# Eight output buffers instead of three, one raw-V buffer instead of two, and relu and output scaling free to run on VectorE or ScalarE, in a fused attention and expert kernel

## The chip, the cores and the metric

The kernel runs on one core of a Trainium2 chip. The metric is the device time of one execution in microseconds (us), as the median of the runs. The span in a profile is about 2 us shorter than the time of the same run. Runs whose time lies over 1.5% above the fastest of the same kernel are marked slow.

A ratio is the mean time of one kernel's fast runs over the mean of the other's fast runs of the same rounds, so it is not quite the quotient of the medians that are quoted.

## The reference, cut to what matters

```python
# q, k, v: (8, 8, 576, 64).  Attention in a window of 32 to each side
scores = scale * q @ k^T;  scores = where(|i - j| <= 32, scores, -1e9)
x = (softmax(scores) @ v)  ->  (8, 576, 512)
# one expert of eight for each of the 8 batches
logits = x.mean(axis=1) @ w_gate          # (8, 8)
e_idx  = argmax(logits)                   # the batch's expert
out[b] = gate_w[b] * (relu(x[b] @ w1[e]) @ w2[e])   # w1: 512x1024, w2: 1024x512
```

The expert is known only when a batch's attention is done, so its weights are loaded in the middle of the work. While they load, the attention of the next batch runs.

## The kernel before

A planner in the kernel simulates the engines with a duration for each piece of work and emits the instructions in the order that it finds. On the chip each engine then works its queue in that order; only what a piece needs makes it wait: its data, a free buffer and, as e8 below shows, the semaphores of transfers. A piece planned for `BOTH` goes to whichever of VectorE (`DVE`) and ScalarE (`ACT`) the planner finds better.

The profile's names: PE is TensorE, PEld its weight load, POOL GpSimd, SP SyncE; ACTq and SPq are the issuing of transfers by ScalarE and SyncE. `bank` is a matmul's result, `qT`, `kT` and `xT` are transposed q, k and attention outputs, `E` the exponentials, `vaug` the V that the attention matmuls read, `vraw` V as it was loaded, `w` the expert's weights, `hT` the hidden layer after relu, `gwb` the gate weight and `osb` the outputs.

```python
vraws = buffers("vraw", [P, NVS + 1, D], FP32, 2)
buffers("osb", [P, DM], FP32, 3)                     # outputs on their way to memory
...
# exponentials (line 468) on ScalarE, masks (474 to 487) on VectorE
plan.add("ACT", 0.63, f"X{sn}", ex, ...)
plan.add("DVE", 0.47 if half == 0 else 0.4, f"M{sn}", msk, ...)
...
# first expert matmul (line 664), 16 times per batch; then relu
nc.scalar.activation(h_of[(b, ft)][:, 288*c : 288*c + 288], bank_of.pop(gn)[:, 0:288], ACTF.Relu)
...
# second expert matmul (lines 700 and 706), 5 outputs per batch; then the scaling (line 726)
nc.scalar.activation(osb[:, 0:w], bank_of.pop(f"2{b}{i}")[:, 0:w], ACTF.Copy,
                     bias=0.0, scale=tiny("gwb", [P, 1], FP32, b))
...
# the store is issued from ScalarE's queue too (line 737)
nc.scalar.dma_start(out[b, 128*i : 128*i + 128, :], osb)
```

The softmax here doesn't subtract the row's maximum and nothing guards it: scores larger than these inputs give would overflow.

## Time and profile before

| | kernel before |
|---|---|
| time, median of 3 runs | 305.97 us (305.24 to 307.08) |
| span of the profiled run | 302.7 us |
| TensorE busy, and so not busy | 231.4 us, 71.3 us |
| mean granted TensorE clock | 0.861 |
| VectorE busy, ScalarE busy | 168.9 us, 163.5 us |

The lines of the profile stand in the prediction.

### The profile page before, as it was taken

How to read it: one execution, taken by the hardware profiler on the slowest of the kernel's cores; microseconds unless marked ns; L12 is line 12 of the kernel's file. 1: busy time of each engine (PE TensorE's matmuls, PEld its weight loads, DVE VectorE, ACT ScalarE, POOL GpSimd, SP SyncE). 2: the span in 40 equal slices, each digit the busy share in tenths (PEclk: the TensorE clock that was granted, in tenths of full speed). 3: DMA queues.
4: the chain of work that ended last, by engine and by line, in shares of the span. 5: the costliest groups of instructions: out<-in, count | busy, mean ns of one | idle time of the engine just before them, and what ended most of it. 6: DMA issues, size and time to landing. Idle time of an engine off the chain costs nothing.

```text
span 302.7 us, 6131 instructions
## 1 busy us (share of the span) xinstructions
PE 231.4 (76%) x2432; PEld 177.3 (59%) x2432; DVE 168.9 (56%) x453; ACT 163.5 (54%) x320; POOL 68.4 (23%) x83
## 2 busy tenths in 40 slices
PE   1475878995899649995699729993599929975990
PEld 1374756854796339854496429852497518833840
DVE  7889992475459735685458925686277525400000
ACT  8692923572578255681577425681466535631640
POOL 4536060091106400091004600082002200010000
PEclk9996975999599958997599958997599977995798
DMA  7879999099997997089942996079101970089021
GB/s 248 281 214 393 298 197 269 30 180 264 348 344 166 241 362 223 1 157 235 384 131 38 241 322 228 2 142 226 68 2 17 212 192 17 2 160 239 35 106 53
DMA packets 26637, 55.00 MB, mean 182 GB/s; under 512 B 2064, under 2 KB 12272, under 8 KB 24560
## 3 DMA queue, kind: packets, MB, share of 16 engines
q0 software_dynamic: 2304, 16.78, 29.4%
q1 hardware_dynamic: 18656, 28.39, 27.5%
q10 hardware_dynamic: 5648, 9.44, 8.5%
q8 instruction: 19, 0.31, 0.4%
q14 instruction: 10, 0.08, 0.1%
HBM read 61.94 MB, written 9.44 MB: 236 GB/s over the span
## 4 chain that ended last, share of the span: by engine, by line
PE 49%; DMA 31%; DVE 8%; ACT 5%; issue 4%; ACTq 0%
DMA out_dram<-osb 28%; PE bank L664 25%; PE bank L700 9%; PE bank L513 5%; PE bank L391 4%; PE bank L549 3%; DMA w<-in_moe_w_dram 3%; ACT E L468 2%; ACT osb L726 2%; PE bank L574 1%; DVE E L487 1%; ACT kT L307 1%; DVE qT L305 1%; PE bank L439 1%; PE bank L596 1%
## 5 line engine op out<-in xcount | busy, mean ns | idle before, releaser
L664 PE MATMUL bank<-xT,w 128*128 128x288 f16 x512 | 90.3, 333 | 12.6 <-ACT osb L726 7.3
L664 PEld LDWEIGHTS <-w 128*128 128x128 f16 x512 | 66.5, 151 | 23.6 <-issue 9.0
L682 ACT ACTIVATE hT<-bank 128x288 f16<-128x288 f32 x128 | 51.8, 411 | 37.0 <-PE bank L664 31.5
L513 PE MATMUL bank<-vaug,E 128*128 128x65 f16 x576 | 33.9, 210 | 39.4 <-ACT E L468 30.2
L700 PE MATMUL bank<-w,hT 128*128 128x512 f16 x256 | 63.6, 379 | 0.0
L726 ACT ACTIVATE osb<-bank,gwb 128x512 f32<-128x512 f32 (+1 forms) x40 | 25.7, 642 | 64.6 <-DMA out_dram<-osb 53.5
L487 DVE TENSOR_TENSOR E<-E,mask 128x384 f16<-128x384 f16 (+1 forms) x64 | 34.6, 550 | 38.9 <-ACT E L468 38.9
L513 PEld LDWEIGHTS <-E 128*128 128x128 f16 x576 | 29.2, 109 | 43.6 <-issue 32.5
L634 POOL DMA_DIRECT2D w<-in_moe_w_dram x8 | 4.7, 585 | 176.8 <-DVE gw L627 135.5
L468 ACT ACTIVATE E<-bank 128x512 f16<-128x512 f32 x72 | 41.1, 596 | 3.5 <-PE bank L439 1.4
L330 POOL CAST qkb<-raw 128x1152 bf16<-128x1152 f32 x32 | 37.7, 1212 | 13.5 <-DMA raw<-in_k_dram 7.4
L305 DVE COPY qT<-bank 64x512 bf16<-64x512 bf16 (+1 forms) x46 | 35.3, 774 | 2.1 <-PE bank L391 0.6
L700 PEld LDWEIGHTS <-hT 128*128 128x128 f16 x256 | 22.8, 98 | 18.3
L391 PE MATMUL bank<-id_bf,qkb 128*128 128x128 bf16 x288 | 25.4, 234 | 10.2 <-POOL qkb L330 7.6
L391 PEld LDWEIGHTS <-qkb 128*128 128x128 bf16 x288 | 20.4, 105 | 15.2 <-POOL qkb L330 8.1
L535 DVE TENSOR_TENSOR xs<-bank,linv 128x256 f16<-128x256 f32 x64 | 27.1, 424 | 2.2
L439 PEld LDWEIGHTS <-kT 128*128 128x128 bf16 x288 | 20.3, 103 | 10.2 <-issue 4.7
L439 PE MATMUL bank<-qT,kT 128*128 128x128 bf16 x288 | 24.6, 230 | 1.9 <-DVE qT L305 1.3
L307 ACT COPY kT<-bank 128x512 bf16<-128x512 bf16 (+1 forms) x26 | 18.4, 736 | 9.7 <-PE bank L391 9.6
L305 DVE COPY xT<-bank 128x512 f16<-128x512 f16 (+1 forms) x23 | 8.8, 384 | 25.9 <-PE bank L549 25.8
L365 POOL CAST vaug<-vraw 128x1152 f16<-128x1152 f32 (+1 forms) x16 | 18.9, 1236 | 6.8 <-DMA vraw<-in_v_dram 6.8
L533 DVE RECIPROCAL linv<-bank 128x4 f32<-128x4 f32 (+1 forms) x80 | 13.9, 174 | 8.6 <-PE bank L513 8.1
(61 smaller groups left out, 176.8 us busy)
## 6 DMA issues: line engine op xcount, KB each, us to landing
w<-in_moe_w_dram POOLq DMA_DIRECT2D x16, 1024.0 KB, 11.9
raw<-in_q_dram SPq DMA_DIRECT2D x16, 576.0 KB, 4.6
raw<-in_k_dram SPq DMA_DIRECT2D x16, 576.0 KB, 9.6
out_dram<-osb ACTq DMA_DIRECT2D x32, 256.0 KB, 10.5
out_dram<-osb ACTq DMA_DIRECT2D x8, 128.0 KB
vraw<-in_v_dram SPq DMA_DIRECT2D x8, 0.2 KB, 11.2
vraw<-in_v_dram SPq DMA_DIRECT2D x8, 8.0 KB, 10.0
vraw<-in_v_dram SPq DMA_DIRECT2D x1, 24.0 KB
```

The lines of the kernel that those rows point to most:

```text
L305: nc.vector.tensor_copy(dst, src)
L330: nc.gpsimd.tensor_copy(t, raw[(b, quad, name)].rearrange("p h j d -> p j h d"))
L391: nc.tensor.transpose(pv[:, j - j0, :], raw[(b, quad, name)][:, j], id_bf)
L439: nc.tensor.matmul(dst, qkT[(b, a, "k")][:, k0 : k0 + P], qkT[(b, a, "q")][:, :, k0 : k0 + 64], start=(m == 0), stop=True, skip_group_chec ...
L468: nc.scalar.activation(dst, src, ACTF.Exp, bias=0.0, scale=0.125)
L487: nc.vector.tensor_tensor(ev, ev, mask[:, 1:2].unsqueeze(1).broadcast_to([P, 2, m, 64]), ALU.mult)
L513: nc.tensor.matmul(bank[:, hp * 65 : hp * 65 + 65], E_of[b][:, h, c0 : c0 + P], va_of[b][:, late, slot, 0:65], start=(hp == 0 and n == 0), ...
L535: nc.vector.tensor_tensor(xv[:, par], hv[:, :, 0:64], linv.to_broadcast([n, 4, 64]), ALU.mult)
L664: nc.tensor.matmul(bank[:, 0:288], w_of[b][0].rearrange("p t (c n) -> p t n c", c=P)[:, dt, ft], xT_of[b][:, dt, 288 * c : 288 * c + 288], ...
L682: nc.scalar.activation(h_of[(b, ft)][:, 288 * c : 288 * c + 288], bank_of.pop(gn)[:, 0:288], ACTF.Relu,)
L700: nc.tensor.matmul(bank, h_of[(b, ft)][:, 128 * i : 128 * i + 128], w2s[:, ft, :], start=(ft == 0), stop=(ft == NFT - 1),)
L726: nc.scalar.activation(osb[:, 0:w], bank_of.pop(f"2{b}{i}")[:, 0:w], ACTF.Copy, bias=0.0, scale=tiny("gwb", [P, 1], FP32, b),)
```

## The change

The intent is to take ScalarE's wait for output stores away with five more buffers, to make room for them by giving up one buffer of raw V, and to let VectorE, which had as much time to spare, take part of relu and scaling. The planner's assumption of how long a store holds its buffer is lengthened as well.

```diff
-                over = end + 2.6
+                over = max(end + 2.6, min(dma_at + 0.7, end + 10.0))
...
-    vraws = buffers("vraw", [P, NVS + 1, D], FP32, 2)
+    vraws = buffers("vraw", [P, NVS + 1, D], FP32, 1)
...
-    buffers("osb", [P, DM], FP32, 3)
+    buffers("osb", [P, DM], FP32, 8)
...
+                    if op.eng == "DVE":
+                        nc.vector.tensor_scalar_max(dst, src, 0.0)
+                    else:
+                        nc.scalar.activation(dst, src, ACTF.Relu)
-                plan.add("ACT", 0.42, "R" + gn, relu,
+                plan.add(BOTH, {"DVE": 0.38, "ACT": 0.42}, "R" + gn, relu,
...
+                if op.eng == "DVE":
+                    nc.vector.tensor_scalar_mul(osb[:, 0:w], src, gwb)
+                else:
+                    nc.scalar.activation(osb[:, 0:w], src, ACTF.Copy, bias=0.0, scale=gwb)
-            plan.add("ACT", 0.69 if i < 4 else 0.43, f"V{b}{i}", evac,
+            plan.add(BOTH, {"DVE": 0.62, "ACT": 0.7} if i < 4 else {"DVE": 0.36, "ACT": 0.44}, f"V{b}{i}", evac,
```

In the changed kernel's profile the second expert matmuls are lines 702 and 708, relu is line 685 (VectorE) and 687 (ScalarE), the scaling 730 and 732, and the store 740 and, for a batch's fifth output, 742.

## The prediction

> **What bounds the kernel now.** I began with the page: the share of each engine, the strip of 40 slices, then the chain that ended last.
>
> ```profile
> PE 231.4 (76%) x2432; PEld 177.3 (59%) x2432; DVE 168.9 (56%) x453; ACT 163.5 (54%) x320; POOL 68.4 (23%) x83
> ...
> PE 49%; DMA 31%; DVE 8%; ACT 5%; issue 4%; ACTq 0%
> DMA out_dram<-osb 28%; PE bank L664 25%; PE bank L700 9%; PE bank L513 5%; PE bank L391 4%; PE bank L549 3%; DMA w<-in_moe_w_dram 3%; ACT E L468 2%; ACT osb L726 2%; PE bank L574 1%; DVE E L487 1%; ACT kT L307 1%; DVE qT L305 1%; PE bank L439 1%; PE bank L596 1%
> ```
>
> No engine is full, TensorE is nearest, and 28% of 302.7 us, about 85 us, is time in which the chain sits on an output store. A store should release nobody in a hurry, so I asked the view of waits who waits for it.
>
> ```profile
> ACT osb L726 <- DMA out_dram<-osb: 53.5, 13, 6.7
> DVE E L487 <- ACT E L468: 38.9, 15, 6.2
> ...
> PE bank L513 <- ACT E L468: 30.2, 9, 5.6
> DVE xT L305 <- PE bank L549: 25.8, 22, 6.2
> ...
> PE bank L664 <- ACT osb L726: 7.3, 4, 2.5
> ...
> PE bank L664 <- ACT hT L682: 0.4, 1, 0.4
> ```
>
> ScalarE stands 53.5 us, in 13 waits, before the output scaling (line 726), because its buffer is still being stored. There are three buffers and five outputs per batch, so outputs 4 and 5 of a batch wait for stores 1 and 2, and a 256 KB store takes a median of 10.5 us to land. ScalarE works in program order, so the exponentials of the next batch (line 468), which have their data, stand behind that wait; VectorE's masks and TensorE's attention matmuls then wait for them. The last line matters as well: TensorE hardly ever waits for relu.
>
> The timeline from 202 to 220 us (the sixth batch's experts start there) shows one such stop. Columns: start, duration, engine, line, operation, and in brackets the idle time before it.
>
> ```profile
> 202.29 0.69 ACT L726 ACTIVATE osb<-bank,gwb 128x512 f32<-128x512 f32 x1 [0.53 <-PE bank L700]
> ...
> 207.99 0.69 ACT L726 ACTIVATE osb<-bank,gwb 128x512 f32<-128x512 f32 x1 [3.94 <-DMA out_dram<-osb]
> ...
> 209.30 0.60 PE L513 MATMUL bank<-vaug,E 128*128 128x65 f16 x8 [2.89 <-ACT E L468]
> ...
> 214.54 0.47 ACT L726 ACTIVATE osb<-bank,gwb 128x256 f32<-128x256 f32 x1 [5.38 <-DMA out_dram<-osb]
> ...
> 215.55 0.60 PE L513 MATMUL bank<-vaug,E 128*128 128x65 f16 x8 [5.65 <-ACT E L468]
> ...
> 215.96 3.50 PE L664 MATMUL bank<-xT,w 128*128 128x288 f16 x16
> ```
>
> TensorE loses 2.89 and 5.65 us, and the first expert matmuls (line 664) start only at 215.96. The same stop comes at every batch. Last, I cut this stretch into windows (columns: start and end, length, busy us per engine, granted clock, DMA share, GB/s).
>
> ```profile
> 205.40:206.40 1.00, 1.00 (x18) 0.84 (x16) 1.00 (x1) 0.00 (x0) 0.61 (x1) 1.00 1.26 285
> 206.40:209.30 2.90, 0.02 (x1) 0.03 (x1) 1.98 (x7) 1.17 (x2) 0.00 (x0) 0.87 1.01 229
> ...
> 211.00:215.50 4.50, 0.00 (x0) 0.00 (x0) 0.00 (x0) 0.96 (x2) 0.00 (x0) 0.50 0.38 135
> 215.50:217.60 2.10, 2.05 (x15) 1.56 (x15) 1.36 (x4) 1.05 (x3) 0.00 (x0) 0.50 0.09 25
> ...
> 219.90:223.00 3.10, 3.10 (x47) 3.06 (x46) 2.42 (x9) 1.94 (x5) 0.00 (x0) 1.00 0.00 0
> ```
>
> The clock falls to 0.50 in the stop and is only back at 1.00 by 220: the stop is paid a second time. It also shows that VectorE was still busy until about 208.3, which limits what can be won.
>
> **What the Trainium skill says.** "TensorE: Matmul & The Clock Gate", Part 1, says that the clock is halved after an idle window of about 3.4 us and full again after about as long a busy one. The trace agrees: 0.50 in the stop, and on the chain 16 matmuls of line 664 take 3.31 us from 216.15 (207 ns each) and 12 take 1.51 us from 220.93 (126 ns each). "DMA: Bandwidth & Descriptors", Issuing engines are not separate DMA queues, says all queues run on the same 16 engines and interleave; so a store shares with the weights and inputs. The trace agrees: 10.5 us median when they run, as little as 2.0 us at best. "VectorE: DVE Perf Modes", Why PSUM operands drop a tier, says an fp32 PSUM operand runs at the plain rate on VectorE. The trace fits: 128x256 out of fp32 PSUM takes 424 ns (line 535) while a 128x512 fp16 copy out of PSUM also takes 424 ns (line 305). So VectorE is no cheaper place for relu or scaling. "SBUF — State Buffer", Who interferes with whom, says VectorE and GpSimd share a port pair that one holds alone. The trace agrees: the mask of line 487 takes 1.30 us at 201.40 beside GpSimd's casts, 0.35 us at 207.56 after them.
>
> **The change part by part.** *Eight output buffers.* Output n waits for store n-8, over a batch back, 30 us against 10 to 13 us of landing: all 53.5 us of these waits should go. What it is worth on the path I read stop by stop, as how much earlier the experts' matmuls could start. Two other things bound that: VectorE's work queue, and the weights, whose first half lands 8.2 to 9.9 us after issue. At 216: masks and copies are done at 208.3, two groups of attention matmuls follow, so the start moves to about 209.5, a gain of 6.4 us; the weights, issued at 197.7, are there by 206.5. At 249 (weights issued at 232.84, landing near 241.6): start near 242, gain 7. At 180: about 6, by likeness. At 148 (eight of these matmuls were done before its second wait): 4.5. At 111 (masks done at 104.3): 5.5. At 76.7 (eight done before): TensorE lost 1.38 and 2.23 us, so 3.7. In the last batch the first eight start at 274.48 when the weights land, which stays; the wait until 277.82 after them goes, about 2.5. Sum 35.6 us of the 53.5.
>
> *Clock.* Six stops are followed by about 16 matmuls at half rate; at 207 to 240 ns instead of 126 that is 1.3 to 1.8 us, six times 8 to 11 us. A pause of some 2 us before the attention matmuls stays (206.4 to 208.5), so I count 6.5 us.
>
> *Relu and scaling on both engines.* 128 relus of 411 ns and 40 scalings of 642 ns are on ScalarE, 77.5 us. On VectorE I estimate, from 424 ns for 256 elements and one element per 0.96 GHz cycle (that clock is the "VectorE: DVE Perf Modes" page's), 157 ns fixed: 457 ns for a relu and 690 ns for a 512-wide scaling. Each moved instruction saves ScalarE what it costs VectorE. TensorE waits 0.4 us for relu, so this alone gives nearly nothing; scaling on VectorE can even get between two masks. I count 0, plus or minus 4 us, as the order of the two queues will be planned anew.
>
> *One buffer for raw V.* The load of V for the next batch must wait for GpSimd's cast of this one. In the steady part the cast comes right after the weights are issued (130.4, 164.5, 199.1 us) and its next one a batch later, so a load of about 11 us has 25 us: hidden. At the start it is not: the second V load is issued at 13.01 us, the first cast ends at 15.9, and SyncE's later loads stand behind it in order. About 3 us of delay in the second batch's casts, where TensorE already waits 5.9 us; I charge 2 us.
>
> Sum: 35.6 + 6.5 - 2 = 40 us, so 306 - 40 = 266 us.
>
> **The rivals.** *The wait was hidden anyway, or the weights take its place.* For: they land on the same saturated DMA engines, and at 274.48 they are already the releaser. Against: at 216 they had 9 us of slack. If all periods were bound by issue to landing, I would gain only some 20 us: 285. *DMA becomes the bound.* The shares of the queues, 29.4 + 27.5 + 8.5% of 302.7 us, are 198 us, 24.7 per batch. Before, a period was about 34 us; at 27 us it is 92% full, and with one V buffer the input loads move into the burst right after the weights' issue. That could cost 1 to 2 us a period: 272 to 280. *VectorE becomes the bound.* It is full from 197.4 to 208.3 already; three scalings of 0.69 us there would delay the masks by 2 us a batch, 14 us in all: 280. Against: the planner puts an instruction where the queue is shorter. *Everything opens up.* All 53.5 us plus 11 of clock: 242 us, but TensorE's 26.6 busy us of the 35.1 us from 193.9 to 229.0 and VectorE's queue speak against it.
>
> **Range and chances.** The stop is real and repeated, and five new buffers remove it without new work, so faster is nearly certain. The two DMA and VectorE rivals pull up more than a better plan pulls down. Predicted 266 us, 8 in 10 between 256 and 281; faster 0.96, same 0.03, slower 0.01.
>
> **What would show it.** In the changed profile the wait of output scaling on its store should be below 3 us and its 28% of the chain gone; TensorE's share should be near 85%, the mean clock above 0.90 (0.861 now), and expert matmuls should start every 27 to 28 us instead of 30 to 36. Some 40 to 70 relus should be VectorE's, near 0.46 us, with their wait still nil. The wait of TensorE for GpSimd's casts near 30 us should grow by about 2. I am wrong if the new plan puts another wait between experts: for weights (first landing above 12 us), or for VectorE.

## More of the kernel before

"Busy" counts the time in which an engine had an instruction running, so a matmul at half the clock counts twice as long as at the full clock. That is why the split of TensorE's span into busy and not busy is worth keeping: lost clock is in the first part, waiting is in the second.

## The result, and the profile after

The changed kernel takes 264.25 us (260.86 to 264.82, 3 runs) against 305.97 us, ratio 0.8578 (95% interval 0.8433 to 0.8722): faster, and within 2 us of the predicted 266. The span is 261.9 us and the mean clock 0.942.

The page of the changed kernel: the engines' shares, then the chain that ended last by engine and by line.

```profile
PE 217.2 (83%) x2432; PEld 170.5 (65%) x2432; DVE 204.9 (78%) x524; ACT 131.7 (50%) x249; POOL 68.0 (26%) x80
...
PE 55%; DVE 26%; DMA 6%; issue 5%; ACT 4%; ACTq 1%; POOLq 1%; DVEq 0%
```

The store, 28% of the chain before, is gone, and the view of waits has no line any more for a scaling that waits for a store. But VectorE, 8% of the chain before, is now 26%. In the view of waits these lines lead to it (engine, line and what it waited for; us in all, times, longest):

```profile
ACT E L468 <- PE bank L439: 14.7, 12, 3.4
...
PE bank L439 <- DVE kT L305: 5.4, 4, 2.3
...
PE bank L513 <- DVE vaug L370: 4.7, 4, 2.0
...
PE bank L513 <- ACT E L468: 2.6, 6, 0.7
```

TensorE's attention matmuls (line 513) waited 30.2 us for exponentials before and wait 2.6 us now. A new chain of waits has come: the score matmuls (line 439) wait for VectorE's copy of k, and ScalarE's exponentials wait for those scores.

The groups of relu and scaling in the changed kernel, shapes kept apart (count, busy us, mean ns, idle before):

```profile
L687 ACT ACTIVATE hT<-bank 128x288 f16<-128x288 f32 x72 | 29.5, 412 | 28.5 <-PE bank L664 26.4
L685 DVE TENSOR_SCALAR hT<-bank 128x288 f16<-128x288 f32 x56 | 25.6, 458 | 20.8 <-PE bank L664 19.9
...
L730 DVE TENSOR_SCALAR osb<-bank,gwb 128x512 f32<-128x512 f32 x19 | 14.2, 746 | 7.9 <-PE bank L702 7.8
...
L732 ACT ACTIVATE osb<-bank,gwb 128x512 f32<-128x512 f32 x13 | 8.9, 683 | 1.7 <-PE bank L702 1.7
```

Both jobs take longer on VectorE than on ScalarE. The planner thinks the opposite: 0.38 us for a relu on VectorE and 0.62 us for a scaling.

The timeline shows what that does around the point where the kernel before had its stop (changed kernel, one period; start, duration, engine, line, operation, idle time before it):

```profile
178.05 1.16 DVE L482 TENSOR_TENSOR E<-E,mask 128x128 f16<-128x128 f16 x1
179.13 1.30 DVE L487 TENSOR_TENSOR E<-E,mask 128x384 f16<-128x384 f16 x1
180.35 0.81 DVE L305 COPY kT<-bank 128x640 bf16<-128x640 bf16 x1
181.09 0.74 DVE L730 TENSOR_SCALAR osb<-bank,gwb 128x512 f32<-128x512 f32 x1
...
181.85 0.34 ACTq L740 DMA_DIRECT2D out_dram<-osb  x1
182.24 1.08 ACT L468 ACTIVATE E<-bank 128x512 f16<-128x512 f32 x2 [3.36 <-PE bank L439]
```

```profile
181.31 0.61 PE L439 MATMUL bank<-qT,kT 128*128 128x128 bf16 x8 [2.33 <-DVE kT L305]
```

VectorE works without a pause through masks, a copy of k and a scaling. TensorE stands 2.33 us for the copy of k, which VectorE had put behind two masks of over a microsecond each (GpSimd's casts run beside them, from 177.86 to 181.44 us). ScalarE stands 3.36 us. The profile names the scores as what ended this wait, but ScalarE's store (line 740) is issued at 181.85, as the scaling on VectorE ends (181.09 plus 0.74 us), and it stands in front of the exponentials in ScalarE's queue.

The same 147 us of both kernels as one window, first before and then changed (start and end, length, busy us of TensorE, weight load, VectorE, ScalarE and GpSimd, then clock, DMA share, GB/s):

```profile
75.00:222.00 147.00, 116.27 (x1282) 90.80 (x1282) 91.32 (x226) 80.96 (x169) 33.76 (x37) 0.84 0.72 201
```

```profile
75.00:222.00 147.00, 136.23 (x1660) 109.84 (x1659) 126.60 (x321) 86.85 (x179) 37.28 (x42) 0.99 0.84 224
```

The clock is at 0.99 instead of 0.84, and TensorE is busy for 136 of 147 us instead of 116. Eleven us are still lost here, and VectorE is the busiest of the other engines.

### The profile page after: what moved, and what is told of

Same layout as the page of the kernel before. It is cut to its first block, busy times and chain, and to the rows that moved or that the text cites. A ratio compares the mean times of both kernels' runs of the same rounds, so it can differ in the third digit from the quotient of the medians.

```text
span 261.9 us, 6135 instructions
## 1 busy us (share of the span) xinstructions
PE 217.2 (83%) x2432; PEld 170.5 (65%) x2432; DVE 204.9 (78%) x524; ACT 131.7 (50%) x249; POOL 68.0 (26%) x80
## 4 chain that ended last, share of the span: by engine, by line
PE 55%; DVE 26%; DMA 6%; issue 5%; ACT 4%; ACTq 1%; POOLq 1%; DVEq 0%
PE bank L664 27%; PE bank L702 10%; DMA w<-in_moe_w_dram 6%; PE bank L513 6%; DVE E L487 6%; DVE qT L305 5%; PE bank L549 3%; DVE E L482 3%; PE bank L439 3%; PE bank L391 3%; DVE kT L305 3%; ACT E L468 2%; DVE osb L730 2%; PE bank L708 2%; PE bank L574 2%
## 5 line engine op out<-in xcount | busy, mean ns | idle before, releaser
L664 PE MATMUL bank<-xT,w 128*128 128x288 f16 x512 | 77.6, 301 | 6.3 <-DMA w<-in_moe_w_dram 6.2
L664 PEld LDWEIGHTS <-w 128*128 128x128 f16 x512 | 62.7, 147 | 9.9 <-DMA w<-in_moe_w_dram 6.6
L687 ACT ACTIVATE hT<-bank 128x288 f16<-128x288 f32 x72 | 29.5, 412 | 28.5 <-PE bank L664 26.4
L685 DVE TENSOR_SCALAR hT<-bank 128x288 f16<-128x288 f32 x56 | 25.6, 458 | 20.8 <-PE bank L664 19.9
L513 PE MATMUL bank<-vaug,E 128*128 128x65 f16 x576 | 29.6, 200 | 13.1 <-DVE vaug L370 4.7
L513 PEld LDWEIGHTS <-E 128*128 128x128 f16 x576 | 25.5, 102 | 16.6 <-issue 13.4
L391 PE MATMUL bank<-id_bf,qkb 128*128 128x128 bf16 x288 | 25.8, 234 | 10.3 <-POOL qkb L330 7.3
L305 DVE COPY qT<-bank 64x640 bf16<-64x640 bf16 (+1 forms) x39 | 30.3, 783 | 1.3 <-ACT qT L307 0.3
L307 ACT COPY xT<-bank 128x512 f16<-128x512 f16 (+1 forms) x26 | 13.6, 528 | 18.4 <-PE bank L549 17.7
L307 ACT COPY qT<-bank 64x512 bf16<-64x512 bf16 (+1 forms) x25 | 18.2, 729 | 9.1 <-DVE qT L305 5.6
L730 DVE TENSOR_SCALAR osb<-bank,gwb 128x512 f32<-128x512 f32 (+1 forms) x21 | 15.2, 721 | 8.4 <-PE bank L702 7.8
```

The source lines that it names most:

```text
L305: nc.vector.tensor_copy(dst, src)
L307: nc.scalar.copy(dst, src)
L391: nc.tensor.transpose(pv[:, j - j0, :], raw[(b, quad, name)][:, j], id_bf)
L513: nc.tensor.matmul(bank[:, hp * 65 : hp * 65 + 65], E_of[b][:, h, c0 : c0 + P], va_of[b][:, late, slot, 0:65], start=(hp == 0 and n == 0), ...
L664: nc.tensor.matmul(bank[:, 0:288], w_of[b][0].rearrange("p t (c n) -> p t n c", c=P)[:, dt, ft], xT_of[b][:, dt, 288 * c : 288 * c + 288], ...
L687: nc.scalar.activation(dst, src, ACTF.Relu)
```

## The experiments

Twelve kernels were run, all with correct results. A kernel with eight output buffers and two V buffers could not be built, because the memory of a partition was over-full by 2.3 KB (210.2 of 207.9), so that corner is missing.

**e1: the buffers alone.** Relu and scaling stay on ScalarE; eight output buffers and one V buffer are kept.

```diff
-                plan.add(BOTH, {"DVE": 0.38, "ACT": 0.42}, "R" + gn, relu,
+                plan.add("ACT", 0.42, "R" + gn, relu,
-            plan.add(BOTH, {"DVE": 0.62, "ACT": 0.7} if i < 4 else {"DVE": 0.36, "ACT": 0.44}, f"V{b}{i}", evac,
+            plan.add("ACT", 0.7 if i < 4 else 0.44, f"V{b}{i}", evac,
```

> Changed kernel with relu and output scaling on ScalarE alone again (eight output buffers and one V buffer kept). Theory A (the prediction's: the buffers carry the gain, the second engine is worth 0 plus or minus 4 us): 260 to 268 us, no wait of ScalarE for an output store, relu wait of TensorE below 2 us. Rival B (ScalarE's queue would have become the next bound, so the second engine is needed): over 272 us, with TensorE's expert matmuls waiting for relu or the exponentials. Rival C (VectorE, now 78% busy and 26% of the chain, is the bound that the move made): below 258 us and VectorE's share of the chain back near 10%.

Measured: 252.18 us (251.35 to 253.61), ratio 0.8256 (0.8203 to 0.8308). The range of theory A, 260 to 268 us, is missed. Theory C holds in the time: without the second engine the kernel is about 12 us faster than the changed one by the medians, and 10 us by the ratios (0.8578 - 0.8256 = 0.0322 of 305 us). On the chain its share for VectorE only falls to 23%, not to 10%, so that part of C was wrong. The page and the window of e1:

```profile
PE 215.7 (86%) x2432; PEld 170.1 (68%) x2432; DVE 167.6 (67%) x453; ACT 163.6 (65%) x320; POOL 68.3 (27%) x80
```

```profile
75.00:222.00 147.00, 142.24 (x1714) 113.85 (x1712) 112.06 (x299) 105.42 (x222) 38.77 (x45) 1.00 0.86 229
```

TensorE is busy 142.24 of 147 us, 97%, at the full clock. There is hardly anything left to be won on other engines in this part.

**e2: the V buffer alone.** The kernel before with one line changed.

```diff
-    vraws = buffers("vraw", [P, NVS + 1, D], FP32, 2)
+    vraws = buffers("vraw", [P, NVS + 1, D], FP32, 1)
```

> Kernel before with one raw V buffer and nothing else. Theory A: the V loads are hidden in the steady part and the start loses up to 2 us: 305 to 309 us, the 53 us of waits for stores unchanged. Rival (the later V loads push the input loads into the weights' landing): over 312 us, and the first half of the weights lands later than 10 us after its issue.

Measured: 303.71 us (303.6 to 305.4), ratio 0.9971 (0.9905 to 1.0037): the same, and a little below the 305 us that were expected at least. The waits of ScalarE for stores are 53.7 us, as before. The start lost nothing either: the first weights were issued at 37.76 us, against 38.23 before. The planner, knowing of one buffer, puts the second batch's loads of q and k in front of its V load. With e1 this is a clean pair: the orders of all five queues of e1 and e2 are identical, and only the number of output buffers differs (8 and 3). So the five buffers by themselves are worth the step from 0.9971 to 0.8256. The planner's longer assumption for a store, which e1 has and e2 has not, changed nothing in this order; what it does when relu and scaling are free was not tested.

**e3 and e4: one of the two jobs on both engines.** e3 frees relu alone, e4 scaling alone; each is the changed kernel with the other job's `plan.add` as in e1.

> Changed kernel with output scaling on ScalarE alone, relu on both engines. Theory A: 260 to 268 us, VectorE busy about 190 us. Rival C: if VectorE's place in front of the masks is what the scaling took, this is faster than the changed kernel by 3 us or more; if relu is what loads VectorE, no difference.

> Changed kernel with relu on ScalarE alone, output scaling on both engines. Theory A: 260 to 268 us. Rival C: about 3 us or more faster than the changed kernel if relu on VectorE is what delays norms and copies; no difference if it is the scaling among the masks.

Measured: e3 253.63 us, ratio 0.8338 (0.827 to 0.8406); e4 259.49 us, ratio 0.8482 (0.842 to 0.8544). Over e1 relu costs 0.8% of the time before and scaling 2.3%; together that is 3.1%, and the changed kernel has 3.2%. So it is mainly the scaling that costs, the job with only 40 instructions: e3 has 55 relus on VectorE and its interval overlaps that of e1, e4 has 25 scalings there and its interval does not. e3 gains what theory C expected if the scaling was at fault; e4 should then not differ from the changed kernel and is 2.9 us better by the ratios, which is within the intervals.

**e5 and e6: queue or plan?** e5 has the plan of e1 to the last instruction, but two scalings of each batch are issued on VectorE at their place in the plan. e6 is the changed kernel with VectorE's durations in the planner set to what the traces show.

```diff
 e5
-                if op.eng == "DVE":
+                if i in (1, 3):
                     nc.vector.tensor_scalar_mul(osb[:, 0:w], src, gwb)
 e6
-    plan.add(BOTH, 0.74 if first else 0.6,                    (copies of q and k)
+    plan.add(BOTH, {"DVE": 0.82, "ACT": 0.75} if first else 0.72,
-    plan.add("DVE", 0.47 if half == 0 else 0.4, f"M{sn}", msk,
+    plan.add("DVE", 1.0 if half == 0 else 0.5, f"M{sn}", msk,
-    {"DVE": 0.38, "ACT": 0.42}                                 (relu)
+    {"DVE": 0.46, "ACT": 0.41}
-    {"DVE": 0.62, "ACT": 0.7} if i < 4 else {"DVE": 0.36, "ACT": 0.44}   (scaling)
+    {"DVE": 0.75, "ACT": 0.69} if i < 4 else {"DVE": 0.48, "ACT": 0.47}
```

> The kernel of run e1 (all relu and scaling planned for ScalarE), but scalings 2 and 4 of each batch are issued on VectorE at the place that the plan gave them; everything else in every queue stays in the same order. Theory Q (the queue itself: a scaling of 0.75 us among masks and copies delays VectorE, which the attention matmuls wait for): 5 us or more slower than e1, 257 us or above. Theory P (the plan: given a choice of two engines, the planner orders all queues differently, with VectorE's durations too short in its model, and that other order is what costs): within 2 us of e1.

> The changed kernel, relu and scaling free to go to either engine, with the planner's durations for VectorE set to what the trace shows (relu 0.46, scaling 0.75, masks 1.0 and 0.5, copies of q and k 0.82 and 0.72 us). Theory P: the loss of some 12 us against e1 mostly goes, 256 us or below. Theory Q: VectorE is still loaded before the masks, 259 us or above.

Measured: e6 253.79 us (250.49 to 255.48), ratio 0.8355 (0.8273 to 0.8436). As theory P expected, the loss mostly goes: by the ratios two thirds of it (0.8578 to 0.8355, of 0.8578 to 0.8256), although 19 scalings and 32 relus still run on VectorE (21 and 56 in the changed kernel). The window of e6 says the same: TensorE's busy time is 4.2 us above the changed kernel's 136.23, of the 6.0 us that e1 is above it.

```profile
75.00:222.00 147.00, 140.39 (x1704) 112.25 (x1702) 121.74 (x318) 91.67 (x198) 38.50 (x45) 1.00 0.86 231
```

What cost the changed kernel most was the plan made with the wrong durations; which of the corrected ones matters was not tested one by one. TensorE's waits for copies of k (5.4 us in the changed kernel) are gone from e6's view of waits, but those of the first expert matmuls for their weights are 10.3 us, against 6.2 in the changed kernel and 5.3 in e1: there the weights begin to take the place of the old waits.

e5 had a median of 263.41 us, but three of its four runs are slow; the fast one took 258.62 us. That is over the 257 us of theory Q, which would mean that a scaling on VectorE at the place meant for ScalarE also costs, but it is one run without a ratio. The profiled run of e5 is a slow one, so only its order is read here: ScalarE's part of the timeline.

```profile
149.91 1.09 ACT L468 ACTIVATE E<-bank 128x512 f16<-128x512 f32 x2
154.74 0.34 ACTq L740 DMA_DIRECT2D out_dram<-osb  x1
155.18 0.47 ACT L732 ACTIVATE osb<-bank,gwb 128x256 f32<-128x256 f32 x1 [4.19 <-DVE E L487]
```

ScalarE stands 4.19 us. The store of the fourth output is next in its queue, and VectorE's scaling of that output runs from 153.96 to 154.71; the store goes out at 154.74. Everything behind it waits, the exponentials included.

**e7 and e8: four and five output buffers**, both with two V buffers, relu and scaling on ScalarE.

> Four output buffers, two V buffers, relu and scaling on ScalarE alone. If a buffer is worth what its wait is: only output 5 of a batch waits, for the store of output 1 issued about 7.5 us before, which lands after 9 to 12 us; so 2 to 4 us per batch, 258 to 272 us. If one more buffer already suffices: 250 to 255 us.

> Five output buffers, two V buffers, relu and scaling on ScalarE alone. Theory A: an output waits for the store of a whole batch before, about 26 us against 12 us of landing, so no wait is left and the time is that of eight buffers, 250 to 255 us. Then the single V buffer was not needed. Rival (the landing can exceed a batch under load): over 257 us with waits for stores on the page.

Measured: e7 259.76 us, its runs spread from 255.07 to 263.04, two of the four marked slow, and no ratio. The two fast runs, 255.07 and 256.78 us, lie between the two ranges expected. Its waits for stores came to 2.1 us in all instead of 2 to 4 us per batch, but the planner had also ordered all queues otherwise, so it does not tell what a fourth buffer is worth. e8: 265.03 us (263.66 to 266.99), ratio 0.8727: the rival's side of the threshold, but not the rival's reason. There are no waits for output buffers. One single stop stands out, at the last output of the second batch; ScalarE in the view of waits, then the timeline:

```profile
ACT E L468 <- DMA vraw<-in_v_dram: 10.5, 1, 10.5
```

```profile
105.59 0.54 ACTq L742 DMA_DIRECT2D out_dram<-osb  x1
106.17 0.60 ACT L468 ACTIVATE E<-bank 128x512 f16<-128x512 f32 x1 [10.52 <-DMA vraw<-in_v_dram]
...
107.12 1.12 PE L664 MATMUL bank<-xT,w 128*128 128x288 f16 x4 [8.48 <-ACT hT L687]
```

The fifth output's store is held until a V load has landed that was issued at 83.03 us and took 22.48 us on the chain, and TensorE stands 8.48 us. The store does not need that data. No view of the profile says why it is held, but the program built from e8's kernel does. Just before this store ScalarE's queue holds a wait for the semaphore DMAHW4 to reach 80, and it is that V load, issued by SyncE, that raises it to 80 when it has landed. The build gives the transfers of SyncE and ScalarE eight such semaphores in turn, and here a store got the one of a slow load. The kernel before has the same queues and the same pair, but there the store's turn came only at 110.04 us. In e11, which follows, the same store shares its semaphore with a load of k and goes out at once, at 95.89 us.

**e11: five buffers and one V buffer.** The plan is that of e1, queue by queue; only the number 8 becomes 5.

> Run e1 with five output buffers instead of eight; every queue has the same order as in e1. If five buffers are enough and e8's loss came from the V load that the plan with two V buffers issues elsewhere: 250 to 255 us, no wait for stores. If eight are needed: 259 us or above.

Measured: 253.09 us (250.7 to 256.69), ratio 0.828 (0.8196 to 0.8365), the same as e1 within the intervals. Five output buffers are enough, one for each output of a batch. What e8 lost came with its two V buffers and the plan that goes with them, not with the number of output buffers. So the single V buffer, which looks free of effect in e2, spared this kernel e8's stop. That the shared semaphore is all of the difference was not tested by a run of its own.

**e9, e10 and e12: the store in another queue.** The stores of outputs scaled on VectorE are issued by SyncE, in e5, in the changed kernel and in e6. The edit of e9 is shown; e10 and e12 go by the engine that the planner chose.

```diff
-                    nc.scalar.dma_start(out[b, 128 * i : 128 * i + 128, :], osb)
+                    (nc.sync if i in (1, 3) else nc.scalar).dma_start(out[b, 128 * i : 128 * i + 128, :], osb)
```

> Run e5 with the stores of outputs 2 and 4, the ones scaled on VectorE, issued by SyncE instead of ScalarE; the order of all other queues is unchanged. Theory S (a store is issued from ScalarE's in-order queue, so a scaling on VectorE makes ScalarE stand still until VectorE has done it, which blocks the exponentials): most of e5's loss against e1 goes, 255 us or below, and ScalarE has no gap that ends when VectorE's scaling ends. Theory Q (0.75 us in VectorE's queue in front of the masks is the loss): 258 us or above, as e5.

> The changed kernel with the stores of VectorE's outputs issued by SyncE; the plan is the same. Theory S: at least half of its 12 us over e1 goes, 258 us or below. Theory Q or P (VectorE's place in the plan): within 3 us of the changed kernel, 261 us or above.

> Run e6 (changed kernel, durations of VectorE in the planner as the trace shows them) with the stores of VectorE's outputs issued by SyncE. If the loss of the changed kernel is the plan made with too short durations plus ScalarE standing behind its store, both are gone here and TensorE alone bounds the steady part: the weights' issues 26.1 us apart as in e1 and e6, 249 to 254 us, a ratio to the kernel before of 0.82 to 0.835. If a second engine for relu and scaling were worth something of its own, it would show here: below 249 us. If VectorE's load itself costs: 256 us or above.

Measured: e9 256.15 us, its fast runs 253.77, 255.4 and 256.9, ratio 0.8426 (0.8345 to 0.8506). That lies between the two thresholds. ScalarE's gap is gone:

```profile
148.42 1.09 ACT L468 ACTIVATE E<-bank 128x512 f16<-128x512 f32 x2
150.44 0.47 ACT L732 ACTIVATE osb<-bank,gwb 128x256 f32<-128x256 f32 x1 [0.93 <-PE bank L708]
```

It stands 0.93 us here instead of 4.19. Against the one fast run of e5 the fast runs of e9 are 1.3% quicker (mean 255.4 against 258.6), which is too thin to size the effect. Against e1 it is still 0.017 slower by the ratio, outside both intervals, so a scaling on VectorE at a place meant for ScalarE costs something even with its store out of the way.

e10 took 260.02 us, between its two thresholds; its ratio, 0.8579 (0.8513 to 0.8645), is to the third digit the changed kernel's. Its median is 4.2 us lower, but that of the kernel before in its call is 2.4 us lower too. In the window from 75 to 222 us TensorE is busy 137.29 us, 1.1 us more than in the changed kernel, and it waits 5.4 us for copies of k in both. So the store behind VectorE can be seen in the changed kernel, and it is not most of what costs it its 10 us; the interval of the changed kernel's ratio, 0.0145 to each side, leaves room for a few us.

e12 took 252.48 us, ratio 0.8375 (0.8313 to 0.8437): no better than e6 and 1.4% slower than e1 by the ratio, which is just over the range expected. It is not quite a clean test of the store: GpSimd waits 30.9 us for loads of k, against 8.4 in e6, and whether that costs anything is not shown; the first expert matmuls wait 10.8 us for weights. With the plan put right, no run shows that a second engine for relu and scaling is worth anything here.

## Why the prediction was right or wrong

The time was right, and the reason named first was right. Two terms of the sum were mis-sized, in opposite directions, and cancelled; that the total came within 2 us is luck. TensorE's busy time and the rest of the span give each term (us):

| | before | e1 (buffers) | changed |
|---|---|---|---|
| span | 302.7 | 251.7 | 261.9 |
| TensorE busy | 231.4 | 215.7 | 217.2 |
| TensorE not busy | 71.3 | 36.0 | 44.7 |

**Eight output buffers, predicted 35.6 us of the 53.5 us of waits.** TensorE's time not busy falls by 71.3 - 36.0 = 35.3 us in e1. Reading each stop for what would have held TensorE anyway gave the right size, and all 53.5 us of waits did go. That it agrees to 0.3 us is luck in part, as the single stops were estimated to half a microsecond (the one at 76.7 us was put down as 3.7 where its two waits make 3.6). The clean pair of e2 and e1 divides the gain as 37.7 us not busy and 12.4 us busy instead of 35.3 and 15.7, so each part is known to some 2 or 3 us.

**Clock, predicted 6.5 us.** This step failed in size. TensorE's busy time falls by 231.4 - 215.7 = 15.7 us with the same 2432 matmuls. The first expert matmuls (line 664) alone go from 90.3 to 76.8 us. I had discounted the estimate of 8 to 11 us because a pause of some 2 us would stay in each period. Pauses of 0.6 to 1.0 us do stay in e1, and the clock of the whole window from 75 to 222 us is nevertheless 1.00. The count of slow matmuls was about right: in the traces 140 of line 664's take over 400 ns before and 37 in e1, 103 fewer against the 6 times 16 counted. But each was dearer: 13.5 us over 103 is 131 ns of busy time, where I had reckoned with 81 to 114 ns (207 to 240 less 126).

**Relu and scaling on both engines, predicted 0 plus or minus 4 us.** This was wrong: it costs some 10 us by the ratios, 10.2 us of span. The estimated durations were near (457 ns for a relu against 458, 690 for a scaling against 746), and TensorE's wait for relu was nil before, as said. What failed is the sentence against the third rival, that the planner puts an instruction where the queue is shorter. It does so by its own durations, and these were too short for VectorE: 1.0 us for the two masks of a first half (385 + 617 ns in the groups of the kernel before) stood in the plan as 0.47.

```profile
L487 DVE TENSOR_TENSOR E<-E,mask 128x384 f16<-128x384 f16 x32 | 19.8, 617 | 0.0
L482 DVE TENSOR_TENSOR E<-E,mask 128x128 f16<-128x128 f16 x32 | 12.3, 385 | 5.9 <-ACT E L468 5.6
```

e6 corrects them and regains two thirds. The rival had sized the loss at 14 us; it came at 10.

**One buffer for raw V, predicted a loss of 2 us.** e2 shows none in the time. I had taken the order of SyncE's queue as fixed, but the planner reordered it. TensorE's wait for GpSimd's casts at the start was to grow by 2 us and is 7.3 us against 7.6.

So the sum was 35.6 + 6.5 + 0 - 2 = 40, and the runs give 35.3 + 15.7 = 51 of span for the buffers and the V buffer together, less 10 for the second engine, 41 in all. Without e1 the agreement of the total would have looked like a confirmation of every term.

**The other rivals.** The weights' first half lands a median of 8.4 us after issue in the changed kernel (8.8 before), and TensorE's wait for it is 6.2 us against 5.0: not a new bound here, though in e6 and e12 it is over 10 us. The DMA share of the window rises from 0.72 to 0.84. **The signs.** The mean clock (0.942), 56 relus on VectorE and the vanished store are as foretold. TensorE's share is 83% for 85%, and weights are issued every 28.1 us ((228.73 - 60.04) / 6) for 27 to 28; in e1 it is 26.2.

The best version that was run is e1, at 252.18 us and a ratio of 0.8256: it takes the buffers and leaves the two jobs on ScalarE.

## What to carry to other kernels

An engine that works in program order and waits for a buffer also holds up all later work whose data is ready; count the outputs of one round against the buffers, and one buffer per output was enough here. A wait that makes no sense by data or buffers can be that of a semaphore which the build shares out among transfers, so read the built program. Moving work to an engine with time to spare can cost more than it brings when a planner places it by durations that the profile does not confirm, so correct the durations first. And a total that agrees says little about its terms: run the parts alone.

## What the Trainium skill lacked or had wrong

- "ScalarE: Activation LUTs", Rules for kernel authors: it says to use VectorE and not ScalarE for relu and multiplication, with the rate in bf16 as its reason, and makes no exception for other inputs. With fp32 inputs from PSUM, the matmuls' memory, it was the other way round: relu on 128x288 took 458 ns on VectorE and 412 on ScalarE, a scaling of 128x512 took 746 and 683 ns.
- No page draws the consequence of an engine's strict queue order for a store whose data another engine makes: in e5 (profiled slow) ScalarE stood 4.19 us in front of such a store, and 0.93 us at the same place when SyncE issued it (e9).
- No page says that a built program can share completion semaphores between the transfers of two issuing engines, so that one transfer waits for an unrelated one: in e8 this held a store, and ScalarE behind it, for 10.5 us.
